# Attention output by column-tiled P V, and a new order of stages, in a fused sliding-attention and gelu-MLP kernel

## The chip, the cores and the metric

One core of one Trainium2 chip. The core has TensorE (matmul into PSUM, eight banks of 128 x 512 fp32), VectorE, ScalarE and GpSimd, each with its own instruction queue that runs in program order, and SyncE, which issues transfers. The metric is the device time of the kernel in microseconds, the median of several executions. Views of the profile come from one further execution, whose span runs from the first to the last instruction.

## The reference, cut to what matters

x is 2048 x 448 in bfloat16. There are 16 heads of 28; each position attends to itself and to seven earlier ones, two apart.

```python
xn = layernorm(x)
q, k, v = split(xn @ wqkv)                  # 448 -> 3 * 448, 16 heads of 28
idx = pos[:, None] - 2 * arange(8)[None]    # W, dil = 8, 2
logits = einsum("bhsd,bhswd->bhsw", q, k[idx]) * 28 ** -0.5   # idx < 0 masked
s = einsum("bhsw,bhswd->bhsd", softmax(logits), v[idx]).reshape(1, 2048, 448) @ wo
h = gelu_tanh(xn @ w1 + b1)                 # 448 -> 1792
g = silu(h @ w2 + b2)                       # 1792 -> 448
out = x + s * g
```

## The kernel before

The kernel writes a list of small tasks with priorities. When it is built, a list scheduler in it fixes the order of the tasks on each engine by costs written in the code; on the chip the order on an engine never changes. Even and odd positions are kept in two halves, so that "two apart" becomes "next to each other".

A sequence of 2048 is cut into 16 tiles of 128 (for projection and MLP), into four chunks of four tiles (F0 to F3 for the first MLP layer, A0 to A3 for attention), and for attention into 17 blocks of 120 or 128 queries, each against 128 keys. Parts that matter here, cut:

```python
# normalisation: 1 / sqrt(var + eps) on GpSimd; tiles 0-3 are turned by TensorE, later ones by SyncE
def rstds(t0, n):
    nc.gpsimd.tensor_scalar(sd, mv[..., 1], eps_t, None, op0=ALU.add)
    nc.gpsimd.tensor_tensor(out=rstd, in0=sd, in1=half_t, op=ALU.pow)
# ...
# attention of block b: four groups hl, each of heads 4*g + hl, g = 0..3
def f1(k):                       # scores: 16 matmuls in 32-row tiles, four banks
    for g in range(G):
        for hl in range(4):
            r = slice(32 * hl, 32 * hl + 32)
            nc.tensor.matmul(buf(p_b, k, hl)[:, g * nq:(g + 1) * nq], qkT[r, 1, g, k0:k0 + P],
                             qkT[r, 0, g, q0:q0 + nq], start=True, stop=True)
# ... per hl: exp on ScalarE (E), times the band mask on VectorE
def f4(k, e=e, hl=hl):           # P V: E turned is the weight, v with a column of ones moves
    for g in range(G):
        h = 4 * g + hl
        nc.tensor.matmul(ps[:, h, :DH + 1], buf(p_E, e)[:, g, :], v[:, h, :DH + 1],
                         start=True, stop=True)
def f5(k):                       # column 28 holds the sums
    nc.vector.reciprocal(rd, po[:, :, DH])
def f6(k):
    nc.vector.tensor_tensor(out=os, in0=po[:, :, :DH], in1=rd.broadcast, op=ALU.mult)
# ... os moved by GpSimd transfers into 128-row tiles ot, each turned by SyncE into oT
# ...
# second MLP layer of a tile: 14 matmuls, then y = bank + b2 (VectorE), tanh (ScalarE),
# g = (tanh + 1) * y (VectorE); final: 4 matmuls oT x wo, sg (VectorE), o = x + sg, store
# ...
# later loads, on GpSimd, each behind a copy that holds the queue
t_hold = hold(w2[:1, 0, :1], w1[:1, 0, :1], t_w1[0], 180)
t_w2 = [dma("POOL", w2[:], B_w2..., 1568, 82, [t_hold])]
# ...
t_b1 = dma_T(b1T[:], lambda: b1r[:], [t_b1r, t_b1z], 104, None)   # b1 turned by SyncE
# ...
t_hold = hold(x_sb[:1, 8:NT, 0], xnT[:1, 0, 8 * P - 1:8 * P].to_broadcast((1, 8)), [t_xT[7]], 180)
load_x(8, 4, 86, "POOL", [t_hold])
load_x(12, 4, 85, "POOL", [t_hold])
# ...
for c, what in ((0, "F"), (0, "A"), (1, "A"), (1, "F"), (2, "A"), (2, "F"), (3, "A"), (3, "F")):
```

exp and gelu need different tables on ScalarE, so the stages are kept apart there: no gelu of a stage runs before the exps of the stage ahead of it.

Of the kernel before, what the change touches and what calls it, by code (L numbers as in the profile page):

```python
# [153 lines left out]
def kernel(  # L154
# [57 lines left out]
    b1r = sb("b1r", [NMT + 2, P])  # L212
    b1T = sb("b1T", [P, NMT + 2])
# [9 lines left out]
    half_t = sb("half_t", [P, 4], F32)  # L223
    m_gen = sb("m_gen", [P, 4, NQ])
# [7 lines left out]
    def ring(name, n, shape, dt=BF16, fifo=False):  # L232
# [4 lines left out]
    p_E = ring("E", 8, [P, 4, P], fifo=True)  # L237
    p_rd = ring("rd", 2, [P, H], F32)
    p_os = ring("os", 3, [P, D])
    p_ot = ring("ot", 4, [P, 512])  # L240
# [16 lines left out]
    FF1 = (((4, 4), (3, 3)),  # L257
           ((3, 3), (2, 2), (2, 2)),
           ((2, 4), (2, 2), (2, 2)),
           ((4, 4), (2, 4)))  # L260
    JOINED = (True, False, True, True)

    PRIO = {
                "project": (118, 114.5, 14, 85.5,),
                "project2": (159, 62.5, 3.5, 2.5,),
                "values": (144, 87, 5.5, 122,),
                "attn": (198.5, 175.5, 115.5, 168, 199, 103.5, 90, 23.5, 117.5, 48, 21.5, 16.5, 199, 155,
            113.5, 27, 19.5,),
                "ff1": (131.5, 199, 127.5, 189.5, 199, 44.5, 146, 190, 145.5, 126, 78, 24.5,),
                "gelu": (72.5, 95, 13, 120,),  # L270
                "ff2": (90, 195, 152, 14.5, 1, 1, 3.5, 1, 43.5, 18.5, 5, 17, 194, 44.5, 75, 5,),
                "final": (33, 2, 153.5, 18, 167, 89, 6, 51, 110, 44.5, 97.5, 119, 122, 5, 119.5, 196.5,),
                "norm": (82.5, 198.5, 165, 80, 21, 39.5, 1, 52, 172, 21, 154, 94.5, 1.5, 110, 1, 1,),
                "stats": (199, 110, 62.5, 6.5, 79, 149.5, 90.5, 45, 22, 1, 117, 84, 1, 1, 1, 1,),
                "turn_x": (37.5, 15.5, 104, 97, 76, 52, 3, 102, 124.5, 192.5, 197, 169, 187, 180, 1, 10,),
                "turn_qk": (81, 170, 41.5, 3, 35, 176, 78.5, 194, 86, 40, 41.5, 112, 198, 169.5, 174.5,
            37,),
                "turn_o": (163, 4, 72, 4.5, 97.5, 21, 1, 21, 25, 11, 3, 43.5, 119.5, 21.5, 94, 19.5,),
                "move_v": (103.5, 33.5, 20.5, 181, 88, 161.5, 58, 74, 158.5, 134.5, 184, 165.5, 51, 152.5,
            193, 26, 199,),  # L280
                "move_o": (196.5, 199, 167.5, 199, 53, 25.5, 73.5, 145.5, 198, 92, 1.5, 100, 111, 150, 24,
            128, 83.5,),
                "copies": (1, 40.5, 143, 22, 87, 82.5, 22.5, 145, 51, 66.5, 16, 16, 12, 95, 126,),
    }
    LATER = {"qk": 53.5, "v": 31, "gelu": -20.5, "exp": 30, "mask": -25, "pv": 60, "recip": 30, "os": 55, "y": 60, "tanh": 32.5, "g": 30, "sg": 1, "o": 2.5}
# [46 lines left out]
    t_os = [plan.add("POOL", 0.1, memset("gpsimd", o[:, D:], 0.0), [t_on], prio=94) for o in p_ot.bufs]  # L332
    t_wo = [plan.add("POOL", 0.45, memset("gpsimd", wo[64:, 3, :], 0.0), [t_on], prio=93)]
    t_E = [plan.add("POOL", 0.1, memset("gpsimd", e[:, :, NQ:], 0.0), [t_on], prio=95) for e in p_E.bufs]

    def dma(eng, dst, src, kb, prio, deps=(), issue=0.5):
        def fn(_):
            {"SP": nc.sync, "ACT": nc.scalar, "POOL": nc.gpsimd}[eng].dma_start(dst, src)
        a = plan.add(eng, issue, fn, [t_on] + list(deps), prio)
        return plan.add("DMA", kb / (270.0 if prio > 93 else 350.0), lambda _: None, [a], prio, tail=1.7)  # L340


    def dma_sb(dst, src, deps, prio, take=(), give=()):
        def fn(k):
            nc.gpsimd.dma_start(dst(k), src())  # L345
        a = plan.add("POOL", 0.55, fn, deps, prio, take=take)
        return a, plan.add("DMA", 0.4, lambda _: None, [a], prio, give=give, tail=1.4)

    def dma_T(dst, src, deps, prio, give, n=1):
        def fn(_):  # L350
            nc.sync.dma_start_transpose(out=dst, in_=src())
        a = plan.add("SP", 1.27, fn, deps, prio)
        return plan.add("DMA", 0.4 + 0.75 * n, lambda _: None, [a], prio, give=(give,) if give else (), tail=0.6 * n)
# [3 lines left out]
    def load_x(t0, n, prio, eng="SP", deps=()):  # L357
        d = dma(eng, x_sb[:, t0:t0 + n, :],
                rows(x_half, t0 * P, n * P).rearrange("(t p) d -> p t d", p=P), 112 * n, prio, deps)
        for t in range(t0, t0 + n):  # L360
            t_x[t] = d
# [5 lines left out]
    load_x(0, 1, 99.9, "SP")  # L367
    load_x(1, 1, 99.9, "ACT")
    t_w = []

    def load_w(kt, prio):
        t_w.append([dma("SP", w_in[:, kt, :], A_wqkv[kt * P:(kt + 1) * P, :], 336, prio)])

    load_w(0, 99.8)
    load_x(2, 2, 99.7, "SP")
    load_w(1, 99.6)
    load_w(2, 99.5)
    tails = A_wqkv[KF:D, :].rearrange("p (w d) -> p w d", d=D)
    t_w.append([dma("SP", w_in3[:64], tails[:, 0:3:2, :], 112, 99.4),
                dma("SP", w_in3[64:], tails[:, 1:3, :], 112, 99.3)])  # L380

    t_b1z = plan.add("POOL", 0.1, memset("gpsimd", b1r[:], 0.0), [t_on], prio=99)
    t_b1r = dma("SP", b1r[:NMT], B_b1.rearrange("(m f) -> m f", f=P), 4, 94.5)
# [4 lines left out]
    def stats(t):  # L388
        def fn(k):
            s = buf(p_st, k)  # L390
            nc.vector.bn_stats(out=s[:], in_=x_sb[:, t, :])  # L391
            nc.vector.bn_aggr(out=mv[:, t, :], in_=s[:])
        k = plan.add("DVE", 0.8, fn, [t_x[t]], prio=PRIO["stats"][t], take=(p_st,))
        k.give = ((p_st, k, 0),)
        t_st[t] = k
# [3 lines left out]
    def rstds(t0, n):  # L399

        def f(_):
            nc.gpsimd.tensor_scalar(sd[:, t0:t0 + n], mv[:, t0:t0 + n, 1], eps_t[:], None, op0=ALU.add)
            nc.gpsimd.tensor_tensor(out=rstd[:, t0:t0 + n], in0=sd[:, t0:t0 + n], in1=half_t[:, :n], op=ALU.pow)
        b = plan.add("POOL", 0.5, f, [t_st[t] for t in range(t0, t0 + n)] + [t_eps], prio=195)
# [6 lines left out]
    t_xT = {}  # L411

    def norm(t, prio):
        def f1(k):
            xn = buf(p_xn, k)
            nc.vector.tensor_scalar(xn[:, :D], x_sb[:, t, :], mv[:, t, 0:1], rstd[:, t:t + 1],
                                    op0=ALU.subtract, op1=ALU.mult)
            nc.vector.tensor_copy(xn[:, D:], xn[:, KF:D])

        a = plan.add("DVE", 0.5, f1, [t_rs[t]], prio, take=(p_xn,))  # L420
        if t >= TPC:
            t_xT[t] = dma_T(xnT[:, :, t * P:(t + 1) * P], lambda: buf(p_xn, a)[:], [a], PRIO["turn_x"][t], (p_xn, a, 0))
            return

        def f2(k):
            xn, tp = buf(p_xn, a), half_bank(buf(p_b, k))
            for kt in range(KT):
                nc.tensor.transpose(tp[:, kt, :], xn[:, kt * P:(kt + 1) * P], ident[:])
        b = plan.add("PE", 0.25, f2, [a, t_ident], prio, take=(p_b,), give=((p_xn, a, 0),), tail=0.15)

        def f3(k):
            copy(k.on, xnT[:, :, t * P:(t + 1) * P], half_bank(buf(p_b, b)))
        t_xT[t] = plan.add(("DVE", "ACT"), (dve(512, 2), act(512)), f3, [b], prio, give=((p_b, b, 0),))
# [34 lines left out]
    def first_batch(tiles, prio):  # L468

        f = []  # L470
        for kt in range(3):
            for i, js in enumerate(tiles):
# [3 lines left out]
                f.append(plan.add("PE", pe(D, len(js)), f1, js[0].deps[:1] + t_w[kt] + f[i:i + 1] * (kt > 0) + f[:1] * (i > 0), prio - 0.1 * i,  # L476
# [109 lines left out]
    def ff2_part(t, cs, n, end, prio):  # L586
        c, j = divmod(t, TPC)
        halves = []
        for i in range(2):
            def f1(k, i=i):  # L590
                ps = buf(p_b, halves[0] if i else k)
                for mt in range(7 * i, 7 * i + 7):
                    nc.tensor.matmul(ps[:, :n], buf(*h_at[(c, mt)])[:, j * P:(j + 1) * P], w2[:, mt, cs],  # L593
                                     start=(mt == 0), stop=(mt == NMT - 1))
            if i:
                last = j == TPC - 1 and end
                halves.append(plan.add(
                    "PE", pe(n, 7), f1, [halves[0]] + [t_h[(c, mt)] for mt in range(7, NMT)]
# [3 lines left out]
            else:  # L602
                halves.append(plan.add("PE", pe(n, 7), f1, [t_h[(c, mt)] for mt in range(7)] + t_w2 + [ff1_last[c]],
# [4 lines left out]
        def f2(k):  # L608
            nc.vector.tensor_tensor(out=buf(p_y, k)[:, :n], in0=buf(p_b, halves[0])[:, :n], in1=b2[:, cs], op=ALU.add)  # L609
        if t == NT - 1:  # L610
            prio += 9
        y = plan.add("DVE", dve(n), f2, [a, t_b2], prio + LATER["y"], take=(p_y,), give=((p_b, halves[0], 0),))

        def f3(k):
            nc.scalar.activation(buf(p_t, k)[:, :n], buf(p_y, y)[:, :n], ACT.Tanh, scale=0.5)  # L615
        th = plan.add("ACT", act(n), f3, [y], prio + LATER["tanh"], take=(p_t,), table=("exp", "gelu"))

        def f4(k):
            nc.vector.scalar_tensor_tensor(out=buf(p_g, k)[:, :n], in0=buf(p_t, th)[:, :n], scalar=1.0,
                                           in1=buf(p_y, y)[:, :n], op0=ALU.add, op1=ALU.mult)  # L620
        t_g[t].append(plan.add("DVE", dve(n), f4, [th, y], prio + LATER["g"], take=(p_g,), give=((p_y, y, 0), (p_t, th, 0))))


    t_oT, ot_at = {}, {}
    ot = [[] for _ in range(NT)]
# [241 lines left out]
```

The softmax here doesn't subtract the row's maximum and nothing guards it: scores larger than these inputs give would overflow.

## Time and profile before

| what | value |
|---|---|
| time, median of 3 (lowest to highest) | 172.52 us (169.94 to 175.38) |
| profiled span | 171.1 us |
| largest groups on TensorE | second layer 46.5 us, first layer 39.1 us, projections 24.5 and 12.1 us |
| P V matmuls, busy | 10.7 us for 240 of 272, 176 ns each as recorded |
| score matmuls, busy | 6.2 us for 256 of 272, 214 ns each as recorded |
| exp on ScalarE | 64 of 580 ns, 31.2 us |
| mask on VectorE | 60 of 399 ns, 21.6 us |
| reciprocal and multiply of a block on VectorE | 256 and 622 ns |
| GpSimd moves of the attention output | 31 of 545 ns |

TensorE is recorded with one row for matmuls and one for weight loads; matmuls overlap in the array, so that a recorded duration is longer than the pitch at which they follow one another. The chain of work that ended last is followed back from the last instruction and tells which engine or transfer set the end at each moment. "idle before <- releaser" says how long an engine stood before an instruction and what it then came after.

### The profile page before, as it was taken

The page shows a single profiled execution, that of the slowest core. Times are in us where ns is not written, and L with a number is a line of the kernel's source. Part 1 is how long each engine was busy: PE and PEld are TensorE (multiplying, and loading weights), DVE is VectorE, ACT ScalarE, POOL GpSimd, SP SyncE. Part 2 cuts the span into 40 slices and gives each one's busy share as a digit, 9 for nine tenths or more (in the row PEclk, how much of TensorE's full clock was granted, in tenths as well). Part 3 has the DMA queues.
Part 4 walks back from the last instruction along what each step waited for, and adds up shares of the span by engine and source line. Part 5 has one row for each costly group of instructions (what it writes and reads, how often), then busy time and mean ns, then how long its engine had stood idle before and what let it go on. Part 6 is the DMA issues. An engine that isn't in the chain of part 4 may idle for free.

```text
span 171.1 us, 3569 instructions
## 1 busy us (share of the span) xinstructions
PE 156.6 (92%) x1313; PEld 77.4 (45%) x1313; DVE 101.9 (60%) x271; ACT 102.7 (60%) x183; POOL 52.1 (30%) x114
## 2 busy tenths in 40 slices
PE   7999999904999999999999999999999999999950
PEld 2644344402454564334445454335555545445640
DVE  4778530039489988965047888004988994605770
ACT  3017778705467878876569696789615879561210
POOL 7748701513015541880061451102220200300020
PEclk9999999975599999999999999999999999999998
DMA  5999999891347777958469897500134121170110
GB/s 150 284 285 250 196 291 204 141 281 47 72 104 151 168 148 97 204 121 119 99 122 171 133 148 130 104 0 25 35 83 110 51 49 40 50 92 0 54 42 13
DMA packets 40701, 20.80 MB, mean 122 GB/s; under 512 B 34144, under 2 KB 38692, under 8 KB 40684
## 3 DMA queue, kind: packets, MB, share of 16 engines
q1 hardware_dynamic: 37372, 13.61, 41.7%
q0 software_dynamic: 3168, 6.85, 16.6%
q8 instruction: 10, 0.16, 0.4%
q10 hardware_dynamic: 144, 0.11, 0.3%
q14 instruction: 7, 0.06, 0.1%
HBM read 7.06 MB, written 1.84 MB: 52 GB/s over the span
## 4 chain that ended last, share of the span: by engine, by line
PE 72%; DMA 15%; issue 3%; DVE 3%; POOL 3%; SPq 0%; DVEq 0%; POOLq 0%
PE bank L593 22%; PE bank L557 16%; DMA w<-in_B_w_dram 12%; PE bank L498 10%; PE bank L700 7%; PE bank L658 4%; PE bank L524 4%; PE bank L560 3%; PE bank L636 3%; DMA x_sb<-in_A_x_dram 3%; PE bank L501 2%; DVE st L391 1%; PE bank L527 1%; DVE y L609 1%; DVE sg L705 0%
## 5 line engine op out<-in xcount | busy, mean ns | idle before, releaser
L593 PE MATMUL bank<-w,h 128*128 128x448 bf16 (+1 forms) x238 | 46.5, 342 | 0.0
L564 ACT ACTIVATE h<-bank,b 128x512 bf16<-128x512 f32 x56 | 34.2, 692 | 12.5 <-PE bank L560 6.5
L557 PE MATMUL bank<-xnT,w 128*128 128x512 bf16 x168 | 39.1, 379 | 0.0
L642 ACT ACTIVATE E<-bank 128x480 bf16<-128x480 f32 (+1 forms) x68 | 33.3, 581 | 9.6 <-PE bank L636 9.4
L345 POOL DMA_DIRECT2D ot<-os x31 | 16.8, 545 | 52.7 <-DVE os L670 38.1
L593 PEld LDWEIGHTS <-h 128*128 128x128 bf16 x238 | 22.3, 98 | 18.7 <-issue 1.0
L345 POOL DMA_DIRECT2D v<-v_tok x30 | 16.3, 549 | 29.2 <-ACT v_tok L303 18.0
L557 PEld LDWEIGHTS <-w 128*128 128x128 bf16 x168 | 15.5, 98 | 20.7 <-issue 3.8
L498 PE MATMUL bank<-w_in,xnT 128*128 128x448 bf16 x96 | 24.5, 380 | 0.1
L650 DVE TENSOR_TENSOR E<-E,m_gen 128x480 bf16<-128x480 bf16 x60 | 21.6, 399 | 1.8 <-ACT E L642 1.6
L615 ACT ACTIVATE t<-y 128x448 f32<-128x448 f32 (+1 forms) x17 | 9.6, 562 | 18.4 <-DVE y L609 18.3
L391 DVE BATCH_NORM_STATS2 st<-x_sb 128x6 f32<-128x448 bf16 x16 | 9.7, 605 | 15.7 <-DMA x_sb<-in_A_x_dram 15.7
L658 PEld LDWEIGHTS <-E 128*128 128x128 bf16 x272 | 11.3, 97 | 13.1 <-DVE E L650 7.1
L609 DVE TENSOR_TENSOR y<-bank,b 128x448 f32<-128x448 f32 (+1 forms) x17 | 10.1, 594 | 9.0 <-PE bank L593 8.6
L665 DVE RECIPROCAL rd<-bank 120x16 f32<-120x16 f32 (+1 forms) x17 | 4.4, 256 | 17.9 <-PE bank L658 17.8
L700 PE MATMUL bank<-wo,oT 128*128 128x448 bf16 (+1 forms) x68 | 14.7, 341 | 0.0
L303 ACT CAST qk_tok<-bank 128x448 bf16<-128x448 f32 x20 | 10.4, 537 | 6.1 <-PE bank L498 2.0
L303 ACT CAST v_tok<-bank 128x448 bf16<-128x448 f32 x13 | 6.6, 549 | 11.9 <-PE bank L527 10.9
L498 PEld LDWEIGHTS <-xnT 128*128 128x128 bf16 x96 | 8.3, 101 | 9.5 <-issue 4.5
L524 PE MATMUL bank<-w_in,xnT 128*128 128x448 bf16 x48 | 12.1, 352 | 0.0
L670 DVE TENSOR_TENSOR os<-bank,rd 120x448 bf16<-120x448 f32 (+1 forms) x17 | 10.6, 622 | 0.5
L658 PE MATMUL bank<-v,E 128*128 128x29 bf16 x240 | 10.7, 176 | 0.0
(64 smaller groups left out, 141.0 us busy)
## 6 DMA issues: line engine op xcount, KB each, us to landing
out_dram<-o SPq DMA_DIRECT2D x15, 112.0 KB, 1.9
w<-in_B_w_dram POOLq DMA_DIRECT2D x1, 1568.0 KB, 13.1
w<-in_B_w_dram SPq DMA_DIRECT2D x2, 672.0 KB, 7.8
w_in<-in_A_wqkv_dram SPq DMA_DIRECT2D x3, 336.0 KB, 6.1
x_sb<-in_A_x_dram POOLq DMA_DIRECT2D x2, 448.0 KB, 5.2
w<-in_B_w_dram SPq DMA_DIRECT2D x4, 112.0 KB, 7.1
x_sb<-in_A_x_dram SPq DMA_DIRECT2D x1, 448.0 KB, 6.6
wo<-in_A_wo_dram POOLq DMA_DIRECT2D x1, 336.0 KB, 5.8
```

Of the source, the lines that this page charges most:

```text
L303: nc.scalar.copy(o, i)
L345: nc.gpsimd.dma_start(dst(k), src())
L498: nc.tensor.matmul(ps[:, :D], xnT[:, kt, cs], w_in[:, kt, which * D:(which + 1) * D], start=start, stop=stop)
L524: nc.tensor.matmul(ps[:, :D], xnT[:, kt, k0:k0 + P], w_in[:, kt, 2 * D:], start=start, stop=stop)
L557: nc.tensor.matmul(ps[:], w1[:, kt, ms], xnT[:, kt, cs], start=start, stop=stop)
L564: nc.scalar.activation(buf(p_h, own, i)[:], buf(p_b, own, i)[:], ACT.Gelu_apprx_tanh, bias=b1[:, mt:mt + 1])
L593: nc.tensor.matmul(ps[:, :n], buf(*h_at[(c, mt)])[:, j * P:(j + 1) * P], w2[:, mt, cs], start=(mt == 0), stop=(mt == NMT - 1))
L609: nc.vector.tensor_tensor(out=buf(p_y, k)[:, :n], in0=buf(p_b, halves[0])[:, :n], in1=b2[:, cs], op=ALU.add)
L642: nc.scalar.activation(buf(p_E, k)[:, :, :nq], buf(p_b, a, hl)[:, :4 * nq].rearrange("p (g q) -> p g q", g=4), ACT.Exp, scale=SCALE)
L650: nc.vector.tensor_tensor(out=E[:, :, :nq], in0=E[:, :, :nq], in1=m[:, :, :nq], op=ALU.mult)
L658: nc.tensor.matmul(ps[:, h, :DH + 1], buf(p_E, e)[:, g, :], v[:, h, :DH + 1], start=True, stop=True)
L700: nc.tensor.matmul(ps[:, :n], oT[:, kt, t * P:(t + 1) * P], wo[:, kt, cs], start=(kt == 0), stop=(kt == KT - 1))
```

## The change

It has five parts.

1. P V is computed with v as the weight and the masked E moving, in tiles of 32 columns: the four heads of a group g fill PSUM partitions 32g to 32g + 31, and the result is the transposed output O^T, with the row sums in row 28 of each 32. So no move and no transpose of the output is needed; wo is loaded in a matching layout with zero rows.
2. The sums are inverted through vector transposes: one of 32 x 32 blocks brings row 28 into a column, a reciprocal of 15 or 16 values per partition follows, a second vector transpose spreads them back, and one multiply writes oT.
3. b1 is turned by TensorE instead of by a SyncE transpose; b2 of the last tile is added by a matmul. The first four tiles take their square root on ScalarE, and their turned copies come in halves.
4. The later loads (x tiles 8 to 15, w2 in two halves) are issued on SyncE after the transposes of xn tiles 4 to 7, without the holding copies. b2 and wo stay on GpSimd.
5. The stages come in the order F0 F1 A0 A1 A2 F2 A3 F3, with new priorities; some output additions may go to GpSimd.

```diff
-            def f4(k, e=e, hl=hl):
-                ps = buf(p_b, pv[0] if hl else k)[:].rearrange("p (h c) -> p h c", h=H)
-                v = buf(*v_at[b]) if v_at[b] else v_tok[k0 // P]
+        def f4(k):
+            v = buf(*v_at[b]) if v_at[b] else v_tok[k0 // P]
+            for hl in range(4):
                 for g in range(G):
-                    h = 4 * g + hl
-                    nc.tensor.matmul(ps[:, h, :DH + 1], buf(p_E, e)[:, g, :], v[:, h, :DH + 1],
-                                     start=True, stop=True)
+                    nc.tensor.matmul(buf(p_b, k)[32 * g:32 * g + 32, hl * nq:(hl + 1) * nq], v[:, 4 * g + hl, :],
+                                     buf(p_E, exps[hl])[:, g, :nq], start=True, stop=True)
 ... (cut)
         def f5(k):
-            nc.vector.reciprocal(buf(p_rd, k)[:nq, :],
-                                 buf(p_b, po)[:nq, :].rearrange("p (h c) -> p h c", h=H)[:, :, DH])
+            nc.vector.transpose(buf(p_dt, k)[:, :4 * nq], buf(p_b, po)[:, :4 * nq])
 ... (cut)
+            nc.vector.reciprocal(buf(p_rd, k)[:, :nq // 8],
+                                 buf(p_dt, d)[:, :4 * nq].rearrange("p (b c) -> p b c", c=32)[:, :, DH])
 ... (cut)
+            nc.vector.transpose(buf(p_dt, d)[:, :4 * nq].rearrange("p (b c) -> p b c", c=32),
+                                buf(p_rd, r)[:, :nq // 8].unsqueeze(2).to_broadcast((P, nq // 8, 32)))
 ... (cut)
+            nc.vector.tensor_tensor(out=oT[:, :, q0:q0 + nq],
+                                    in0=buf(p_b, po)[:, :4 * nq].rearrange("p (l q) -> p l q", l=4),
+                                    in1=buf(p_dt, d)[:, :4 * nq].rearrange("p (l q) -> p l q", l=4), op=ALU.mult)
 ... (cut: rstds of tiles 0 to 3)
+                nc.scalar.activation(sd[:, t0:t0 + n], mv[:, t0:t0 + n, 1], ACT.Sqrt, bias=eps_t[:])
+                nc.vector.reciprocal(rstd[:, t0:t0 + n], sd[:, t0:t0 + n])
 ... (cut: the second layer of the last tile)
+                if biased and not i:
+                    nc.tensor.matmul(ps[:, :n], row0[:], b2[:, cs], start=True, stop=False)
 ... (cut: b1)
-    t_b1 = dma_T(b1T[:], lambda: b1r[:], [t_b1r, t_b1z], 104, None)
+        nc.tensor.transpose(half_bank(buf(p_b, k))[:, 0, :], b1r[:], ident[:])
 ... (cut: loads)
-    t_hold = hold(x_sb[:1, 8:NT, 0], xnT[:1, 0, 8 * P - 1:8 * P].to_broadcast((1, 8)), [t_xT[7]], 180)
-    load_x(8, 4, 86, "POOL", [t_hold])
-    load_x(12, 4, 85, "POOL", [t_hold])
+    turned = [t_xT[t].deps[0] for t in range(TPC, 2 * TPC)]
+    load_x(8, 4, 86, "SP", turned)
+    load_x(12, 4, 85, "SP", turned)
+    t_w2 = [[dma("SP", w2[:, 7 * i:7 * i + 7, :], B_w2[F // 2 * i:F // 2 * (i + 1), :].rearrange("(m p) c -> p m c", p=P),
+                 784, PRIO["loads"][4], turned, 1.0)] for i in range(2)]
 ... (cut)
-    for c, what in ((0, "F"), (0, "A"), (1, "A"), (1, "F"), (2, "A"), (2, "F"), (3, "A"), (3, "F")):
+    for c, what in ((0, "F"), (1, "F"), (0, "A"), (1, "A"), (2, "A"), (2, "F"), (3, "A"), (3, "F")):
```

With another order the list scheduler lays out the engines anew, so nearly every instruction changes its place.

## The prediction

> **What bounds the kernel now.** I read the summary of engines and the 40 slices first, then busy time by stretch, then the chain that ended last, then what the waiting engine and the SyncE queue did in that stretch.
>
> ```profile
> PE 156.6 (92%) x1313; PEld 77.4 (45%) x1313; DVE 101.9 (60%) x271; ACT 102.7 (60%) x183; POOL 52.1 (30%) x114
> ...
> PE   7999999904999999999999999999999999999950
> ...
> PEclk9999999975599999999999999999999999999998
> ```
>
> TensorE is busy 92% of the span. The one hole is in slices 9 and 10, and the granted clock falls with it. By stretch (us; busy time and count of PE, PEld, DVE, ACT, POOL; then the clock):
>
> ```profile
> 7.60:32.30 24.70, 24.59 (x153) 10.91 (x151) 11.67 (x36) 14.89 (x24) 9.71 (x19) 1.00 1.09 238
> 32.30:40.80 8.50, 1.81 (x24) 0.81 (x23) 3.80 (x11) 2.50 (x6) 3.42 (x6) 0.76 0.71 186
> 40.80:46.86 6.06, 6.06 (x33) 2.58 (x34) 3.55 (x10) 4.02 (x9) 0.85 (x1) 0.50 0.24 48
> 46.86:164.10 117.24, 117.24 (x1066) 59.16 (x1064) 76.59 (x187) 79.62 (x144) 31.34 (x57) 1.00 0.52 95
> ```
>
> From 46.86 to 164.10 TensorE never pauses and has full clock; there VectorE is busy 76.59 of 117.24 us, 65%. From 40.80 to 46.86 it runs at clock 0.50. The hole itself, in the chain (start, duration):
>
> ```profile
> 13.66 13.10 DMA w<-in_B_w_dram
> ...
> 31.59 0.22 POOL x_sb L739
> 31.81 0.33 issue
> 32.14 4.63 DMA x_sb<-in_A_x_dram
> 36.86 0.64 DVE st L391
> ...
> 40.41 0.34 DVE E L650
> 40.80 0.29 PE bank L658 x4
> ```
>
> and in the time-ordered views of VectorE, TensorE and the SyncE queue:
>
> ```profile
> 36.86 0.63 DVE L391 BATCH_NORM_STATS2 st<-x_sb 128x6 f32<-128x448 bf16 x1 [13.65 <-DMA x_sb<-in_A_x_dram]
> 40.80 0.29 PE L658 MATMUL bank<-v_tok,E 128*128 128x29 bf16 x4 [6.69 <-DVE E L650]
> 17.93 7.74 SPq L351 DMA_TRANSPOSE qkT<-qk_tok  x1
> ```
>
> TensorE waits 6.69 us for a mask that VectorE could have applied near 33.0 (exp was running from 32.39). VectorE executes in order and had stood 13.65 us at the statistics of x tile 8. That tile was late because its load sat on GpSimd behind a one-element copy that waits for the turned xn tile 7; the transposes of that on SyncE started only at 28.96, since one q/k transpose ahead of them held the queue 7.74 us while the 1568 KB w2 load was in flight (13.66 to 26.76). So the hole is a chain of queue order, not a lack of engines.
>
> **What the skill says.** "DMA: Bandwidth & Descriptors", section "Issuing engines are not separate DMA queues": issues from any engine share the same 16 DMA engines, and another issuer saves only issue time. The trace agrees: the SyncE transpose stretched from a median issue of 1.28 to 7.74 us beside GpSimd's load. So "later loads on SyncE" is worth its order, not bandwidth. "TensorE: Matmul & The Clock Gate", Part 1: an idle window of about 3.4 us drops the array to half clock. The trace agrees: 6.69 us idle, then 0.50. "TensorEngine Tiling (Array Packing)", section "Key Properties": different tiles load and multiply in parallel, but changing the mode drains the array. The trace has it for row tiles: 16 score matmuls, each recorded with 211 ns, take 0.32 us in the chain. It has no column tile, and the page adds under "Restrictions and Gotchas" that column tiling disables fast weight load. "VectorE: DVE Perf Modes", "Why PSUM operands drop a tier": fp32 from PSUM runs 1x. The trace: 448 fp32 from PSUM 621 ns, 448 bf16 in SBUF 390 ns. No run here shows a vector transpose.
>
> **The change, part by part.**
>
> *Order of stages and loads.* With F0 F1 first, TensorE has 84 + 28 feed-forward matmuls before the first score, and needs neither x tiles 8 to 15 nor w2 until late. x is issued on SyncE right after the transposes of xn 4 to 7, then w2 in two halves. x tile 4's load order is as before, its statistics began at 14.97, xn was ready at 21.05 to 23.2. Without w2 in flight the transposes should issue at their normal 1.2 us each, the last landing near 27 (2.5 us each). TensorE reaches F1 at: first projection near 7, projection of four tiles about 9.4 (36 matmuls of 0.19, 6 tail pairs of 0.19, 16 turns, drains), F0 10.8 (42 x 0.2155, 7 tail pairs, drains), so 27: about equal. x then lands near 31, w2's halves near 35 and 37, wanted near 36 and 43. The hole of 6.69 us goes. Of the 6.06 us at half clock, the work was four projection groups of three at 0.57 (2.28), 16 P V matmuls (0.39) and four tails (0.48), each at what it takes elsewhere in the chain: 3.15 us at full clock; 2.9 us go as well. Sum 9.6.
>
> *P V in column tiles.* Now 17 x 16 matmuls of 29 columns: 16 take 0.40 us (144.69 to 145.10 in the trace), 6.9 us in all. After: 16 matmuls of 32 x 120, shaped like the scores turned round; if four column tiles run side by side as row tiles do, 0.32 with drains, 5.4 us. Gain 1.5; the biased last tile and the turning of b1 by TensorE cost 0.25 back. Net 1.25.
>
> *Normalisation.* Removed: 17 reciprocals at 0.256 and 17 multiplies at 0.622, 0.88 per block; 31 moves on GpSimd (16.8 us) and 16 oT transposes on SyncE with 3.5 us to landing. None of these is on the chain. Added on VectorE per block: transpose 480 fp32 from PSUM, reciprocal of 15, transpose 480 back, multiply. I charge the three wide ones at 0.65 (0.621 scaled by 480/448) and 0.2 for the small one, with hops 2.2. Extra 1.3 x 17 = 22 us of VectorE work, less 5 output adds moved to GpSimd (0.39 each) and two y: about 121 busy instead of 101.9. It is off TensorE's path unless a stage fills up. That stage is A0 A1 A2. In the changed instruction order its TensorE part holds 105 second-layer matmuls, 90 projection matmuls with 30 tails, 192 score, 160 P V and 20 output matmuls: 50.7 + drains = 51.3 us. The VectorE part up to the last mask of A2 holds 48 masks at the pitch of 0.34 (16.5), 10 whole chains at 2.2 (22), 22 operations of 448 at their pitch of 0.53 (11.7), 3 adds (0.9): 51.1. Equal, with ScalarE 44. Nothing is hidden there any more, so I charge 2 us of new waits. In A3 and F3 VectorE has 39 us against 58.
>
> *Start and end.* Square root on ScalarE instead of a GpSimd power (0.31 + 0.58 per tile), copies of half tiles: the first projection comes 1.2 us earlier than 7.66, but then meets w_in's third slice, which lands later; I count 0.7. At the end, one addition of 0.39 with its hop leaves the chain: 0.45.
>
> **Sum.** Span 171.1 - 6.7 - 2.9 - 1.25 - 0.7 - 0.45 = 159.1, plus 2 of new waits = 161.1. The cross-check from work: TensorE has 147.5 us at full clock now (26.45 to 34.11, 3.15, 117.24, 0.7), 146.2 after; start 7, end tail 5.8: 159.0. The median time 172.52 stands 1.4 over the profiled span, so 162.5; since my VectorE pitches are on the high side for operations that follow one another without a wait, I take 161.5.
>
> **Rivals.** (a) *VectorE becomes the bound in A0 to A2.* For: 51.1 against 51.3, both in order, and each P V bank is held 2.2 instead of 0.9 us while scores want four of eight banks. Against: finals and y can slip into the later stages, which have 19 us of slack. It would give waits of 6 to 8 us, perhaps with a clock drop, and 166 to 169. (b) *Column tiles don't overlap*: one after another with their weight loads, 16 take at least 16 x 0.05 (120 columns at the 0.19/448 of a projection), more likely 1.0 us; 0.6 more per block than now, 10 us, on TensorE's path throughout: 172. For: no fast weight load, no trace of it. Against: the row-tile record and the skill's page. (c) *The hole only moves*: F1 waits for xn 4 to 7 because the q/k transposes lie ahead of them on SyncE behind the w1 loads. For: the same queue did it before. Against: no 1568 KB load is under way then. 2 to 5 us, and 164 to 167. (d) *All dense*, no new wait, column tiles at 0.25: 158 to 159.
>
> **Range and chances.** The certain part (hole and half clock, 9.6 us or 5.6%) is more than 2% by itself; losing it needs (b), or (a) and (c) together. The three times of before spread from 169.94 to 175.38, which widens both ends. Range 156 to 168; faster by over 2% (under 169.1) 0.91, within 2% 0.06, slower 0.03.
>
> **What would show it.** TensorE dense from about 7 to 153, clock 1.00 throughout, no idle of over 3 us; VectorE busy 119 to 123; vector transposes at 0.6 to 0.7; a P V group of 16 at about 0.3; statistics of x tile 8 before 33. Wrong if transposes take over 0.8, if P V takes 0.8, or if TensorE waits on oT multiplies or masks for more than 4 us in total between 44 and 95.

## The result, and the profile after

The changed kernel takes **159.69 us** (median of 4, 159.24 to 160.04), beside 171.88 us for the kernel before on the same chip: a ratio of **0.936**, 95% interval 0.929 to 0.943. The profiled span fell from 171.1 to 158.0 us, the mean granted clock rose from 0.966 to 0.997. The prediction was 161.5 us, with 156 to 168 as its range. The execution whose profile of before is shown took 172.78 us, a little over the median, so that spans show a gain of 13.1 us where the medians show 12.2.

The page of the changed kernel, busy time of each engine and the rows of 40 slices for TensorE and its clock:

```profile
PE 152.3 (96%) x1303; PEld 72.3 (46%) x1310; DVE 117.9 (75%) x292; ACT 107.0 (68%) x199; POOL 35.6 (22%) x69
...
PE   6999999999999999999999999999999999999990
...
PEclk9999999999999999999999999999999999999998
```

The hole of slices 9 and 10 is gone, and so are the 7 and two 5s of the clock. VectorE has 16 us more work than before and is still at 75%. By stretch (start and end in us, length, then busy time and count of PE, PEld, DVE, ACT and POOL, then clock, DMA share, GB/s):

```profile
43.00:95.00 52.00, 52.00 (x590) 24.41 (x589) 45.20 (x98) 41.71 (x86) 14.41 (x25) 1.00 0.49 101
46.40:103.40 57.00, 56.95 (x601) 26.12 (x600) 52.13 (x113) 44.97 (x91) 14.52 (x25) 1.00 0.44 92
...
152.00:158.00 6.00, 2.12 (x23) 1.87 (x20) 3.01 (x9) 0.71 (x2) 0.00 (x0) 0.93 0.17 54
```

From 43 to 95, most of A0 to A2 and the stage the prediction feared, TensorE is busy all 52.00 us while VectorE has 45.20. VectorE isn't through then: TensorE goes on to the first layer of F2 at 97.40, and VectorE's last masks of A2 run from 100.73 to 103.36. Its whole part, which the prediction counted, is the second stretch, from its first mask to its last: 52.13 us. Between the first projection and the last matmul TensorE pauses for some 0.6 us in all. In the time-ordered views of TensorE, VectorE and the SyncE queue:

```profile
7.07 0.54 PE L521 MATMUL bank<-w_in,xnT 128*128 128x448 bf16 x2
97.40 1.46 PE L580 MATMUL bank<-xnT,w 128*128 128x512 bf16 x5
27.47 0.63 DVE L396 BATCH_NORM_STATS2 st<-x_sb 128x6 f32<-128x448 bf16 x1 [7.21 <-DMA x_sb<-in_A_x_dram]
100.73 2.63 DVE L682 TENSOR_TENSOR E<-E,m_gen 128x480 bf16<-128x480 bf16 x8
18.48 5.17 SPq L352 DMA_TRANSPOSE xnT<-xn  x4
23.70 1.13 SPq L339 DMA_DIRECT2D x_sb<-in_A_x_dram  x2
```

With w2 no longer in flight, the four transposes of the turned xn issue in 5.17 us, x tiles 8 to 15 follow at 23.70, and the statistics of tile 8 start at 27.47 instead of 36.86. VectorE still waits for them, 7.21 us, but TensorE has F1 to do. The new operations (groups by line and shape: count, then busy us and mean ns):

```profile
L700 DVE STREAM_TRANSPOSE dt<-bank 128x480 f32<-128x480 f32 x16 | 10.9, 678 | 9.7 <-PE bank L691 9.5
L704 DVE RECIPROCAL rd<-dt 128x15 f32<-128x15 f32 x16 | 4.0, 251 | 0.6
L709 DVE STREAM_TRANSPOSE dt<-rd 128x480 f32<-128x480 f32 x16 | 10.8, 676 | 0.4
L714 DVE TENSOR_TENSOR oT<-bank,dt 128x480 bf16<-128x480 f32 x16 | 10.5, 654 | 0.3
L691 PE MATMUL bank<-E,v 128*32 128x120 bf16 x240 | 5.7, 219 | 0.0
```

**Where the 13.1 us of span came from.** TensorE's idle time in the span fell from 14.5 us (171.1 - 156.6) to 5.7 (158.0 - 152.3): 8.8 us. Its busy time fell by 4.3. The idle time can be laid out: the hole 6.69 to nothing; the tail from the last matmul to the end of the span 6.28 to 3.88; the start ahead of the first projection and the small gaps together 1.5 to 1.8. The busy time: 2.9 us of half clock by the prediction's count, some 0.4 us less work ahead of the first projection, and about 1.0 us left for P V and the small parts on TensorE.

The tail holds a surprise. The last operations on VectorE and on GpSimd, before:

```profile
163.52 1.18 POOL L710 TENSOR_TENSOR o<-x_sb,sg 128x448 bf16<-128x448 bf16 x1 [15.34 <-DVE sg L705]
...
166.03 0.28 DVE L710 TENSOR_TENSOR o<-x_sb,sg 128x224 bf16<-128x224 bf16 x1
```

and after:

```profile
129.38 1.34 POOL L742 TENSOR_TENSOR o<-x_sb,sg 128x448 bf16<-128x448 bf16 x1 [16.27 <-DVE sg L736]
...
155.31 0.27 DVE L742 TENSOR_TENSOR o<-x_sb,sg 128x224 bf16<-128x224 bf16 x1
```

From the last matmul to the last VectorE operation it is 1.49 us before and 1.46 after: nothing gained. But from there to the end of the span it is 4.8 us before (171.1 - 166.31) and 2.4 after (158.0 - 155.58), though the last store's packets take the same time. The last packets of the store are seen before 167.5 of 171.1, and before 156.8 of 158.0.

### The profile page after: what moved, and what is told of

Same layout as the page of the kernel before. It is cut to its first block, busy times and chain, and to the rows that moved or that the text cites. A ratio compares the mean times of both kernels' runs of the same rounds, so it can differ in the third digit from the quotient of the medians.

```text
span 158.0 us, 3488 instructions
## 1 busy us (share of the span) xinstructions
PE 152.3 (96%) x1303; PEld 72.3 (46%) x1310; DVE 117.9 (75%) x292; ACT 107.0 (68%) x199; POOL 35.6 (22%) x69
## 4 chain that ended last, share of the span: by engine, by line
PE 96%; DVE 1%; issue 1%; DVEq 0%
PE bank L620 28%; PE bank L580 23%; PE bank L521 12%; PE bank L731 8%; PE bank L547 6%; PE bank L583 5%; PE bank L319 4%; PE bank L668 3%; PE bank L691 3%; PE bank L524 2%; PE bank L550 1%; PE bank L445 1%; DVE sg L736 1%; DVE o L742 0%; DVE g L652 0%
## 5 line engine op out<-in xcount | busy, mean ns | idle before, releaser
L580 PE MATMUL bank<-xnT,w 128*128 128x512 bf16 x161 | 37.8, 380 | 0.6 <-issue 0.3
L521 PE MATMUL bank<-w_in,xnT 128*128 128x448 bf16 x96 | 22.0, 354 | 0.0
L700 DVE STREAM_TRANSPOSE dt<-bank 128x480 f32<-128x480 f32 (+1 forms) x17 | 11.6, 681 | 10.0 <-PE bank L691 9.9
L648 ACT ACTIVATE t<-y 128x448 f32<-128x448 f32 x15 | 8.7, 588 | 11.3 <-DVE y L642 11.3
L304 ACT CAST qk_tok<-bank 128x448 bf16<-128x448 f32 x29 | 14.2, 541 | 2.4 <-ACT h L587 0.9
L742 POOL TENSOR_TENSOR o<-x_sb,sg 128x448 bf16<-128x448 bf16 x5 | 5.4, 1096 | 32.3 <-DVE sg L736 32.3
L547 PE MATMUL bank<-w_in,xnT 128*128 128x448 bf16 x48 | 12.0, 353 | 0.0
L709 DVE STREAM_TRANSPOSE dt<-rd 128x480 f32<-128x480 f32 (+1 forms) x17 | 11.5, 678 | 0.4
L714 DVE TENSOR_TENSOR oT<-bank,dt 128x480 bf16<-128x480 f32 (+1 forms) x17 | 11.2, 657 | 0.4
L642 DVE TENSOR_TENSOR y<-bank,b 128x448 f32<-128x448 f32 x15 | 9.3, 617 | 2.1 <-PE bank L620 1.9
L430 DVE TENSOR_SCALAR xn<-x_sb,mv,rstd 128x448 bf16<-128x448 bf16 x16 | 6.6, 411 | 4.0 <-DMA xnT<-xn 2.2
```

The lines of the kernel that those rows point to most:

```text
L304: nc.scalar.copy(o, i)
L521: nc.tensor.matmul(ps[:, :D], xnT[:, kt, cs], w_in[:, kt, which * D:(which + 1) * D], start=start, stop=stop)
L547: nc.tensor.matmul(ps[:, :D], xnT[:, kt, k0:k0 + P], w_in[:, kt, 2 * D:], start=start, stop=stop)
L580: nc.tensor.matmul(ps[:], w1[:, kt, ms], xnT[:, kt, cs], start=start, stop=stop)
L700: nc.vector.transpose(buf(p_dt, k)[:, :4 * nq], buf(p_b, po)[:, :4 * nq])
L709: nc.vector.transpose(buf(p_dt, d)[:, :4 * nq].rearrange("p (b c) -> p b c", c=32), buf(p_rd, r)[:, :nq // 8].unsqueeze(2).to_broadcast((P ...
```

## The experiments

The changes were undone or done one at a time, from both ends: e1 and e5 start from the kernel before, all others from the changed one. Part 3 of the change (b1, b2 and the start) was not undone by itself. Ratios are to the kernel before, run beside each, and leave out executions of either kernel that took over 1.5% more than its fastest.

**e1: the loads of x alone, in the kernel before.** x tiles 8 to 15 are issued on SyncE right behind the w1 loads, and their holding copy goes; stages, b1, w2 and P V stay.

```diff
     # behind the last w1 load on SyncE
+    for t0 in (8, 12):
+        nc.sync.dma_start(x_sb[:, t0:t0 + 4, :], rows(x_half, t0 * P, 4 * P)...)
     # on GpSimd
-    t_hold = hold(x_sb[:1, 8:NT, 0], xnT[:1, 0, 8 * P - 1:8 * P]..., [t_xT[7]], 180)
-    load_x(8, 4, 86, "POOL", [t_hold]); load_x(12, 4, 85, "POOL", [t_hold])
```

> The kernel before with one thing changed: x tiles 8 to 15 are issued on SyncE right behind the w1 loads, not on GpSimd behind the holding copy; every other instruction keeps its place. Theory (the hole is queue order): x tile 8 lands near 20 us instead of 36.9, VectorE reaches the first mask near 33, the hole of 6.7 us and the 2.9 us of half clock go; w2 lands up to 3 us later and costs about 2. Time 172 less 8, so 162 to 166, clock 1.00. Rival (the gain of the changed kernel comes from the attention output, which is relieved of moves and transposes): the hole moves to the next wait and the time stays above 169.

Measured: 169.21 us (167.47 to 169.48), ratio 0.983 (0.976 to 0.991), span 167.3. The old hole is gone, but there is a new wait. TensorE and the SyncE queue in order of time, and the waits:

```profile
26.05 5.08 PE L557 MATMUL bank<-xnT,w 128*128 128x512 bf16 x15 [4.45 <-ACT h L564]
10.88 1.85 SPq L743 DMA_DIRECT2D x_sb<-in_A_x_dram  x2
12.89 1.18 SPq L351 DMA_TRANSPOSE b1T<-b1r  x1
...
DVE b L806 <- DMA b1T<-b1r: 6.2, 1, 6.2
ACT L564 <- DVE b L806: 6.8, 1, 6.8
```

The time is where the rival expected it, but the attention output isn't the reason. b1 is turned by a SyncE transpose, which now stands behind the x loads. The first gelu waits for b1, the first layer for banks. So the loads cannot be moved up freely as long as b1 is turned in that queue. The prediction had the turning of b1 by TensorE only as a cost; what it gains in the change, where the loads stand later in the queue, was not tried.

**e5: the same, with the x loads behind b1's transpose.** One line's place differs from e1; nothing else of the change is in it.

> As the first run (the kernel before, x tiles 8 to 15 on SyncE early), but the two x loads stand behind the SyncE transpose of b1 instead of ahead of it. There the x hole was gone and TensorE stood 4.45 us for a gelu that waited for b1. Theory (two waits of one queue, x and b1, each as long as what stands ahead of it): both waits go, w2 lands some 3 us later than before and may cost up to 2; 161 to 165, no TensorE wait of over 2.5 us. Rival (loads pushed ahead always delay something else that TensorE needs, the total of DMA work is what counts): 167 or more, with a new wait on the q/k transposes or on w2.

Measured: 162.68 us (two at 162.68, one at 162.67, one at 174.78), ratio 0.951 (0.939 to 0.964), span 161.0. Why the last took so long isn't known. The stretches that held the hole and the half clock before:

```profile
7.60:32.30 24.70, 24.70 (x154) 11.12 (x153) 14.51 (x44) 15.29 (x25) 12.00 (x21) 1.00 1.11 281
32.30:40.80 8.50, 8.50 (x113) 4.54 (x112) 7.76 (x21) 7.89 (x18) 0.62 (x1) 1.00 0.52 107
40.80:46.90 6.10, 6.10 (x75) 3.13 (x71) 5.57 (x17) 4.82 (x11) 3.36 (x7) 1.00 0.76 161
...
153.00:161.00 8.00, 1.92 (x20) 1.66 (x18) 2.93 (x9) 0.78 (x2) 1.18 (x1) 0.87 0.10 30
```

TensorE is busy throughout at full clock. The place of two load instructions, with the holding copy gone, is worth 10.1 of the 13.1 us of span, with the old stages and the old P V; by the ratios it is 4.9 of 6.4%, about three quarters as well. The old long tail is still there: 8.00 - 1.92 = 6.08 us.

**e2: the old loads in the changed kernel.** w2 whole and x tiles 8 to 15 go back to GpSimd behind the holding copies; all else is the change, with its order on every engine.

```diff
+    t_hold = hold(w2[:1, 0, :1], w1[:1, 0, :1], t_w1[0], 180)
+    t_w2 = [[dma("POOL", w2[:], B_w2..., 1568, 82, [t_hold])]] * 2
+    t_hold = hold(x_sb[:1, 8:NT, 0], xnT[:1, 0, 8 * P - 1:8 * P]..., [t_xT[7]], 180)
-    load_x(8, 4, 86, "SP", turned); load_x(12, 4, 85, "SP", turned)
+    load_x(8, 4, 86, "POOL", [t_hold]); load_x(12, 4, 85, "POOL", [t_hold])
```

> The changed kernel with only the later loads as before: w2 whole on GpSimd from about 13 us behind a copy that waits for w1, x tiles 8 to 15 on GpSimd behind a copy that waits for the turned xn tile 7; every engine else keeps its order. Theory (queue order of loads is what counts): the q/k transposes on SyncE stretch beside w2 again, xn tiles 4 to 7 are turned near 30 to 35 us instead of 18.5 to 23.7, F1 wants them at 25.3, so TensorE stands 6 to 9 us there and runs at half clock after it: 168 to 172. Rival (the new order of stages hides the late x by itself): 159 to 162.

Measured: four times spread from 168.0 to 175.94 us, median 174.56, too wide for a ratio; span 172.0 in the execution traced, of 173.68. TensorE and the SyncE queue in order of time, and then the same three transposes in the changed kernel:

```profile
39.57 4.76 PE L584 MATMUL bank<-xnT,w 128*128 128x512 bf16 x15 [12.78 <-DMA xnT<-xn]
12.45 15.69 SPq L356 DMA_TRANSPOSE qkT<-qk_tok  x3
```

```profile
13.11 5.28 SPq L352 DMA_TRANSPOSE qkT<-qk_tok  x3
```

Three q/k transposes hold the SyncE queue for 15.69 us beside the w2 load, which took 17.1 us to land, and for 5.28 us without it. The transposes of xn tiles 4 to 7 come behind them, at 28.23, F1 needs those, and TensorE stands 12.78 us in this execution, about twice the old hole. The new order of stages doesn't hide the old loads: even the fastest of the four, 168.0, is 8.3 us above the changed kernel. How large the hole is in that one isn't known. This is the prediction's rival (c), which was said to need w2 in flight.

**e10: the old stage order in the changed kernel.** F0 A0 A1 F1 A2 F2 A3 F3, with the gates between exp and gelu that go with it, and priorities sought anew by search over the kernel's own list scheduler.

```diff
-    for c, what in ((0, "F"), (1, "F"), (0, "A"), (1, "A"), (2, "A"), (2, "F"), (3, "A"), (3, "F")):
+    for c, what in ((0, "F"), (0, "A"), (1, "A"), (1, "F"), (2, "A"), (2, "F"), (3, "A"), (3, "F")):
```

> The changed kernel with the stage order of before (F0 A0 A1 F1 A2 F2 A3 F3), order on each engine sought anew. Theory: with the loads on SyncE the stage order is worth a few us at most (x is there in time, TensorE finds work in either order): 160 to 165 us. Rival: attention blocks in a row from 7 us after the first stage leave TensorE waiting for the exponentials and for VectorE's normalisation, and F1 first is what hides them: 166 us or more.

Measured: 162.07 us (161.2 to 163.16), ratio 0.947 (0.941 to 0.954), span 159.5, no wait of TensorE over 0.83 us after the start. The traced execution is the fastest of the four: the order of stages is worth 1.5 us by the spans and 2.4 by the medians when the loads are right, and the two intervals of the ratios meet.

**e3 and e9: the old P V and its way to O^T in the changed kernel.** Query-major P V, reciprocal and multiply on VectorE, moves by GpSimd, turned by SyncE, wo in its old layout. e3 keeps the change's priorities; in e9 they were sought anew.

```diff
-                    nc.tensor.matmul(buf(p_b, k)[32 * g:32 * g + 32, hl * nq:(hl + 1) * nq], v[:, 4 * g + hl, :],
-                                     buf(p_E, exps[hl])[:, g, :nq], start=True, stop=True)
+                    nc.tensor.matmul(ps[:, h, :DH + 1], buf(p_E, e)[:, g, :], v[:, h, :DH + 1],
+                                     start=True, stop=True)
... (cut: reciprocal, multiply, moves and SyncE transposes as before)
```

> The changed kernel with the old attention output alone: E as weight, 17 x 16 matmuls of 29 columns, reciprocal and multiply, moves on GpSimd, oT turned by SyncE; loads, stages, b1, b2 and start as changed. The scheduler lays the order out anew with the changed priorities, which were not made for it. Theory (loads and stages carry the gain, column tiles 1.5 us of TensorE): 161 to 165, the excess over 1.5 being waits of the untuned order. Rival (the attention output carries it): 168 or more.

> The changed kernel with the old attention output (query-major, moved by GpSimd, turned by DMA), as in the run before of that kind, but now the order of the work on each engine is sought anew for it, so that an end wait of 4.7 us from an order that was made for other work need not be there. Theory: the attention output itself is worth little, the column tiles' 1.4 us of TensorE time and some waits: 161 to 164 us. Rival: it is worth 6 us or more on any order, because the move and the DMA transposes of the last tile always stand ahead of the output projection: 166 us or more.

Measured: e3 168.53 us (168.36 to 168.99), ratio 0.982 (0.976 to 0.988); e9 162.3 us (160.84 to 164.08), ratio 0.942 (0.933 to 0.950). TensorE's longest wait in e3, and in e9:

```profile
161.67 1.68 PE L739 MATMUL bank<-wo,oT 128*128 128x224 bf16 x8 [4.68 <-DMA oT<-ot]
```

```profile
29.08 3.40 PE L560 MATMUL bank<-xnT,w 128*128 128x512 bf16 x15 [1.98 <-DMA xnT<-xn]
```

e3 alone would have said that the new P V is worth 9 us. Half of that is one wait, for the last turned tile, in an order made for a kernel without moves and transposes. With an order of its own (e9) that wait is gone. e9's span of 161.4 stands 3.4 over the changed kernel's: TensorE is busy 1.1 us longer (153.4), and idle 2.3 us longer, most of it the 1.98 us for turned xn at 29.08, which is a wait of loads and transposes and not of P V. So P V in column tiles is worth about 1.1 us of TensorE time, and, in an order that is tuned either way, at most 3.4. The three executions of e9 that count in the ratio have spans of 159.1, 159.7 and 161.4, so the traced one gives the most.

**e4: the four matmuls of one column tile in a row.** The loops over g and hl are exchanged, so that four matmuls in succession go to the same 32 columns.

```diff
-            for hl in range(4):
-                for g in range(G):
+            for g in range(G):
+                for hl in range(4):
```

> The changed kernel with the two loops of P V swapped, so that four matmuls in a row go to the same 32-column tile instead of four different ones; same 16 matmuls, same bank, same order otherwise. If four column tiles run side by side now (my reading of 0.32 to 0.34 us per group of 16 in the chain), one tile at a time costs at least 16 x 0.05 = 0.8 us per group, 0.5 to 0.7 more, times 17 on TensorE's path: 167 to 171. Rival (no overlap of tiles, the group is short because 32-column weights load fast): unchanged, 159 to 160.5.

Measured: 159.72 us (159.63 to 160.32), ratio 0.931 (0.924 to 0.938). A P V group in the chain that ended last, of the changed kernel and of e4:

```profile
57.80 0.33 PE bank L691 x16
```

```profile
57.34 0.35 PE bank L691 x16
```

The other groups differ by 0.02 to 0.03 us too: the order of issue hardly matters. Since this was expected to be the test of overlap and showed nothing, either the tiles overlap in any order, or overlap isn't what makes them fast. e6 decides.

**e6: all sixteen P V matmuls into the first column tile.** Only the first 32 partitions of O^T are written, each over again; three quarters of the attention output are left out, everything after it runs as before.

```diff
-                    nc.tensor.matmul(buf(p_b, k)[32 * g:32 * g + 32, hl * nq:(hl + 1) * nq], v[:, 4 * g + hl, :],
+                    nc.tensor.matmul(buf(p_b, k)[0:32, hl * nq:(hl + 1) * nq], v[:, 4 * g + hl, :],
```

> The changed kernel with all 16 P V matmuls of a block sent to the first 32-column tile, so that the four groups overwrite each other and three quarters of O^T are left out (the normalisation reads what the bank held before); number, size and order of instructions unchanged. Swapping the loops changed nothing, which may mean that tiles queue separately or that tiles play no part. If tiles overlap: 16 x 0.05 = 0.8 us or more per group instead of 0.33, TensorE's path 8 to 10 longer, 167 to 170. If tiles play no part: 159 to 160.5.

Measured: 169.99 us (169.46 to 170.4, 20 runs), ratio 0.994 (0.992 to 0.996), span 168.7 at clock 1.0. That is 10.3 us more, 0.6 us for each of 17 groups, the size that rival (b) had worked out for tiles that don't overlap. A group in the chain shows the same, 0.94 us against 0.33:

```profile
65.51 0.94 PE bank L691 x16
```

The column tiles do overlap, and four in a row to one tile (e4) don't prevent it.

**e7 and e8: more work for VectorE.** One (e7) or two (e8) vector transposes of 480 fp32, 0.68 us each by the trace of the others, are added after each block's multiply; nothing reads them.

```diff
+            for _i in range(1):        # e8: range(2)
+                nc.vector.transpose(idle[:], eps_t[:].to_broadcast((P, 480)))
```

> The changed kernel with one more vector transpose of 480 fp32 (a constant into a spare tile) behind each block's multiply, 0.68 us x 17 on VectorE and nothing else. VectorE is busy 45.2 of the 52 us of A0 to A2; 12 more of 0.68 make 53.4. Theory (VectorE has 6.8 us of slack there, output adds and y can slip): 159.5 to 161.5. Rival (it is at its bound already, each block's chain sets TensorE's pace): 163 or more.

> The same with two more transposes per block, 1.36 us x 17: VectorE's work of A0 to A2 becomes 61.5 us against 52 of TensorE. Theory (VectorE then is the bound of that stage and of A3): 166 to 172, TensorE idle 6 to 12 us. Rival (work slips into F2 and F3): under 163.

Measured: e7 161.65 us (161.29 to 162.08), ratio 0.945 (0.938 to 0.953); e8 173.08 us (172.63 to 173.17), ratio 1.012 (1.004 to 1.020). Both are a little above what the theories expected. The first 17 x 0.68 = 11.6 us of work cost 2.0 us, the second 11.6 cost 11.4. So about 9.6 us of VectorE time were free in the changed kernel, and beyond them each microsecond costs one. That VectorE is then the bound shows in e8 from 60 to 95, inside A0 to A2, where it is busy 34.07 of 35.00 us and TensorE 32.08:

```profile
60.00:95.00 35.00, 32.08 (x330) 14.59 (x329) 34.07 (x72) 23.65 (x50) 11.85 (x21) 1.00 0.64 116
```

Rival (a) was the right danger: it was 10 us away, not next door.

**e11 and e12: less warm-up, and the end rearranged.** Of the 25 warm-up matmuls only the nine wide ones are left, and the output projection of the last tile's first half allowed ahead of the second half's second layer; e12 has its priorities sought anew as well.

```diff
-        t_warm = plan.add("PE", 0.43 if i < 9 else 0.06, fn, [t_warm], -1, take=(p_b,), limit=8.0)
+        t_warm = plan.add("PE", 0.43 if i < 9 else 0.06, fn, [t_warm], -1, take=(p_b,), limit=4.8)
...
-        a = plan.add("PE", pe(n, KT), f1, t_oT[t] + t_wo + [t_f2[t]], prio, take=(p_b,), tail=0.15)
+        a = plan.add("PE", pe(n, KT), f1, t_oT[t] + t_wo + [own], prio, take=(p_b,), tail=0.15)
```

> The changed kernel with fewer warm-up matmuls ahead of the first turned tile (9 wide ones and few narrow), and the output projection of the last tile's first half allowed ahead of the second half's second layer. Theory: the first projection starts 0.2 to 0.5 us sooner, and the end is shorter by 0.2 to 0.4: 159.0 to 159.5 us beside 159.7, ratio to the kernel before 0.925 to 0.935. Rival: fewer warm-up matmuls leave the clock low at the start and the first stage pays more than it gains: 160 us or more.

> As the trimmed kernel, with the order of the work on each engine sought anew. Theory: TensorE is already filled from start to end, so a new order changes little: 158.5 to 160 us. Rival: the new order meets waits that the plan does not see, as other untuned orders did: 161 us or more.

Measured: e11 159.3 us (159.05 to 159.51), ratio 0.931 (0.926 to 0.935), span 157.3; e12 159.83 us (159.03 to 161.39), ratio 0.935 (0.930 to 0.941). e11's first projection starts 1.02 us sooner, at 6.05, but is held twice, 0.39 us for its turned tile and 0.27, at 8.53, for w_in. The mean clock is still 1.0 with less warm-up. The median is 0.4 us under the changed kernel's, but the two were not run side by side and their ranges meet, so it is the best time here rather than a version shown to be faster. Another search, e12, found nothing better.

## Why the prediction was right, step by step

**Hole and half clock, 9.6 us predicted: right.** It is the whole of what decides the sign, and e5 isolates it: 10.1 us of span for moving the loads of x alone. The chain that the prediction read, mask behind statistics behind a load behind a holding copy behind a stretched transpose, is cut at the load in e5, and the stretching of transposes beside the w2 load shows in e2. The prediction put the new stage order into the same term; e5 needs none of it, and e10 gives it 1.5 to 2.4 us. And it passed over b1's place in the SyncE queue (4.45 us in e1).

**P V, 1.25 us net: right.** A group takes 0.32 to 0.37 us in the chain where 0.32 was assumed, e9 gives about 1.1 us of busy TensorE time, and e6 shows that it rests on the overlap.

**New waits in A0 to A2, 2 us: wrong, and the main error.** None arose. The sum of VectorE's work was good: the same 113 operations that the prediction counted (48 masks, ten chains of four, 22 operations of 448, three additions) are busy for 52.13 us, from 46.40 to 103.40, where 51.1 were predicted. TensorE's part took 53.6 us, from 43.85 to 97.40, where 51.3 were predicted. The step that failed is the one from these sums to a wait: "Nothing is hidden there any more, so I charge 2 us of new waits". It takes the end of the stage as one that both engines must reach together. But TensorE went on at 97.40 with the first layer of F2, which needs no mask, while VectorE's last eight masks of A2 ran at 100.73, and their P V followed at 106.76 without a wait for them. Rival (a) had said that finals and y can slip into later stages; here masks did. e7 and e8 measure the room another way, 9.6 us over the kernel.

**Start, 0.7 us: right in size.** The first projection begins at 7.07 instead of 7.66. The wait for w_in, by which the prediction limited it, doesn't show in this trace; e11, which starts sooner, has 0.27 us of it.

**End, 0.45 us: the reason was wrong and the size too small.** The step "one addition of 0.39 with its hop leaves the chain" gained nothing: 1.49 against 1.46 us. The addition is gone, but the last product g, whose tanh ended at 153.76, starts only at 154.40, behind two operations of the tile's first half in VectorE's order. The end of the span came 2.4 us sooner after the last operation, for a reason outside that chain. It is told of below.

So the sum without waits, 159.1, against a span of 158.0, has these errors: the end 1.95 us better than assumed, small gaps of TensorE that grew by 0.47 (0.11 to 0.58) where none were assumed, the start 0.1 worse, and, as the remainder, P V some 0.25 worse, together 1.1. The rest of the miss of 3.1 is the 2 us of waits. From span to time the prediction added 1.4 us, but it took the median and the span from two different executions; within one execution it is 1.7 (172.78 - 171.1 before, 159.74 - 158.0 after).

## What to carry to other kernels

Follow an idle stretch of the busiest engine back to the instruction queue where a load waits its turn: here the place of two loads was worth about three quarters of the gain, and the rewritten computation about one us. When a part of a change is undone in a kernel whose order was tuned for it, tune again before reading its worth (168.5 against 162.3 us here). When work is added to an engine off the critical path, a sum that fills the stage doesn't yet mean a wait: ask whether its last work can run under the next stage. Adding idle work in steps measures the margin.

## What the runs showed of the hardware that was not expected

- **The end of a span after GpSimd's last operation.** In the three kernels whose last GpSimd operation is an output addition shortly ahead of the end (before, e1, e5), the span ends 6.2 to 6.4 us after that operation, and 4.6 to 4.8 us after VectorE's last. In the others, where GpSimd finished at least 9 us before the end, it ends 2.4 to 3.1 us after VectorE's last. It fits a fixed time that GpSimd needs to finish after late work, some 2.2 us of span here. That wasn't tried by itself, and these three are also the only ones with the code of the kernel before, so another difference may be behind it. The cause stays open.
- **Column tiles.** Sixteen matmuls with 128 rows, 32 columns and 120 moving columns take 0.32 to 0.37 us in four tiles, 0.35 to 0.40 when issued tile by tile, and 0.94 in one tile. Two groups in succession take 0.53, so an estimate is 0.21 for the matmuls of a group and 0.11 for going into the tiling and out of it.
- **An addition on GpSimd stretches some of VectorE's work beside it.** In the changed kernel two bfloat16 operations of VectorE, with both inputs in SBUF, ran beside an addition on GpSimd: a mask took 0.97 us where one takes 0.41 on average, and an addition 1.22 us where the others take 0.39. The GpSimd addition beside the second took 1.34 us (shown above, at 129.38), the others about 1.04.

```profile
65.32 1.04 POOL L742 TENSOR_TENSOR o<-x_sb,sg 128x448 bf16<-128x448 bf16 x1
65.67 0.97 DVE L682 TENSOR_TENSOR E<-E,m_gen 128x480 bf16<-128x480 bf16 x1
...
129.75 1.22 DVE L742 TENSOR_TENSOR o<-x_sb,sg 128x448 bf16<-128x448 bf16 x1
```

The fp32 transpose and multiply that ran beside another GpSimd addition (84.62) kept their 0.68 and 0.66 us. e4 repeats both stretches (1.02 and 1.22 us), and e12 has two masks of 1.21 and 1.27 us. No run isolates it, but it eats most of the saving: VectorE has four such additions fewer than before (10 against 14), an estimated 1.6 us, and the two stretches cost 1.4.
